# Sliding-window attention with a soft mixture of experts: P normalised at the head of the next round, in front of the masked copy, the store of x directly behind the bias

## The chip, the core and the metric

The kernel runs on one core of a Trainium2 chip. Its engines are TensorE (PE in the profile; its weight loads are PEld), VectorE (DVE), ScalarE (ACT), GpSimd (POOL) and SyncE (SP, which issues most DMAs). Each engine takes its own instructions in the order in which the program has them and waits on semaphores for the others. The metric is the time of one execution in microseconds (us), as the median of several runs; before the change it is 286.43 us (three runs, 285.88 to 286.63).

## What is computed

First causal attention with a window of 128 keys and a bias that falls linearly with distance, for 8 batches of 576 rows and 8 heads of 64 columns; then, with x the attention's output as 4608 rows of 512 columns, a soft mixture of 8 experts with 4 slots each.

```python
scores = scale * q @ k^T                           # scale = 1/8
scores = where(0 <= rel < 128, scores - slope[h] * rel, -1e9)
attn = exp(scores - max(scores))
attn = attn / (sum(attn) + 1e-9)                   # P
x = (attn @ v)                                     # to 4608 x 512

logits = x @ phi                                   # 32 slots
d = softmax over rows of logits                    # slot inputs: d^T @ x
slot_out[e] = relu(slot_input[e] @ w1[e]) @ w2[e]
return softmax over slots of logits @ slot_out
```

## The kernel before

**Rounds.** A batch's 576 rows are four tiles of 128 and one of 64. A full tile is worked in two groups of four heads, the tile of 64 in one. That makes 9 groups a batch and 72 in all (`groups`); `number` gives a group's place. The front part of the kernel is one loop with a round for each group (round 0 to round 71). It is a software pipeline: in round i the scores of group i+1 are multiplied, the softmax of group i is taken, group i-3 is transposed and group i-4 is multiplied with v. The order on every engine is the order of the code (`manual_schedule`); no scheduler moves anything.

**The steps of a round, by engine.** In the letters that the prediction uses:

- DVE: the masked copy **M** (`merge`, L286) folds the 192 score columns of a block of 64 rows to the 128 of the window. `rowmax` (L300), the reciprocal of the row sums of the group before (`inverse`, L313) and `bias` (L304, written b) follow. **N** (`normalise`, L317) multiplies the four 128x128 blocks of P, all in SBUF, by the reciprocals `rs`. **X** (`x_store`, L424) copies a finished tile of x from PSUM (`xp`) to SBUF. X occurs once a tile, so in about every second round.
- ACT: copy of the transposed P out of PSUM (`split`, L380), sometimes `x_keep` (L447), then the exponentials of the round's group (`expo`, L359), which wait for b.
- POOL: the row sums plus epsilon (`total`, L309), and two `affine_select` on the transposed P, **A** (L386, part that meets the previous tile's keys) and **B** (L388, own keys). Both read and write SBUF.
- PE: transposes (`flip`, L374), **V** (`values`, L410: first the part that needs A, then the part that needs B), scores of the next group (L261 and L270), and now and then the transposes of x, the logits and so on.

**The extra work.** Tiles are collected in passes of four. A pass adds, in the rounds behind it, some DVE work that stands at the end of a round, or in front of the next masked copy: `token_max` (L469), `token_sum` (L496, L498), `slots_max` (L536, L537) and `slot_add` (L522, L524).

**What sets the order around the change.** `softmax_front(new, old)` writes M, rowmax, inverse, b and N of a round, in this order. X and the extra work come later in the loop's body, so on DVE a round ends with N, then X where there is one, then the extra work. `xp` is one PSUM buffer: V of the next tile waits until X has read the last one. P has three SBUF buffers (`p4s`); the reciprocals are in tiles from a pool with two buffers. The first rounds are shorter in depth: `SKIP` is 7, and in round 7 no group is transposed.

Of the kernel before, what the change touches and what calls it, by code (L numbers as in the profile page):

```python
# [10 lines left out]
F32 = mybir.dt.float32  # L11
# [13 lines left out]
P = 128  # L25
# [20 lines left out]
SKIP = 7  # L46
# [18 lines left out]
def bc(ap, dim, n):  # L65
    ap = ap.unsqueeze(dim)
    shape = list(ap.shape)
    shape[dim] = n
    return ap.to_broadcast(shape)
# [3 lines left out]
def tile_attn_softmoe(  # L73
# [16 lines left out]
    work = ctx.enter_context(tc.tile_pool(name="work", bufs=2))  # L90
# [53 lines left out]
    st = {}  # L144
    last = B - 1

    def order(b):
        return (1, 2, 3, 4, 0) if b == last else range(NT)
# [13 lines left out]
    groups = [(b, t, g) for b in range(B) for t in order(b) for g in range(2 if t < 4 else 1)]  # L162
    number = {key: i for i, key in enumerate(groups)}
    n = len(groups)
# [111 lines left out]
    ALL, LO, HI = slice(0, 4), slice(0, 2), slice(2, 4)  # L276
    EVEN, ODD = slice(0, 4, 2), slice(1, 4, 2)

    def merge(key, us=ALL):
        x = ranges(key, us).rearrange("p a (x y) -> p a x y", y=KB)  # L280
        m = x.shape[1]
        if key[1] < 4:
            to, of, keep = x[:, :, 0:6:5], x[:, :, 2:4], bc(mask.bitcast(I32), 1, m)
        else:
            to, of, keep = x[:, :, 0:8:4], x[:, :, 2:8:4], bc(bc(mask[:, 0].bitcast(I32), 1, 2), 1, m)
        nc.vector.copy_predicated(to, keep, of)  # L286

    def ranges(key, us):
        if number[key] == 0:
            return st[key]["parts"][us.start // 2].unsqueeze(1)  # L290
        return st[key]["s4"]
# [4 lines left out]
    def rowmax(key, us):  # L296
        if "nb" not in st[key]:
            st[key]["nb"] = work.tile([P, 4], F32, tag="nb", name="nb")
        st[key]["mx"] = ranges(key, us)[:, :, 4 * P - 2:4 * P]
        nc.vector.tensor_reduce(st[key]["mx"], merged(key, us), axis=AX.X, op=ALU.max, negate=True)  # L300

    def bias(key, us):
        nb = st[key]["nb"][:, us].rearrange("p (a u) -> p a u", u=2)
        nc.vector.tensor_scalar_mul(nb, st[key]["mx"], SCALE)  # L304

    def total(key, us, eng=None):
        if "rs" not in st[key]:
            st[key]["rs"] = work.tile([P, 4], F32, tag="rs", name="rs")
        (eng or nc.vector).tensor_scalar(  # L309
            st[key]["rs"][:, us], st[key]["sm"][:, us], EPS, 1.0, op0=ALU.add, op1=ALU.mult)  # L310

    def inverse(key, us):
        nc.vector.reciprocal(st[key]["rs"][:, us], st[key]["rs"][:, us])  # L313

    def normalise(key, us):
        p4, rs = st[key]["p4"][:, us], st[key]["rs"][:, us]
        nc.vector.tensor_tensor(p4, p4, bc(rs, 2, P), op=ALU.mult)  # L317

    def normalise_first(key, us):
        p4 = st[key]["p4"]  # L320
        for u in range(4)[us]:
            nc.scalar.mul(p4[:, u], p4[:, u], st[key]["rs"][:, u:u + 1])  # L322
# [3 lines left out]
    def filler():  # L326
        if fillers:
            fillers.pop(0)()

    def softmax_front(new, old):  # L330
        first, eager = number[old] == 0, 0 < number[old] < EAGER
        merge(new)
        filler()
        if not eager:
            total(old, ALL, nc.gpsimd)
        if first:
            inverse(old, ALL)
            normalise_first(old, LO)
        rowmax(new, ALL)
        filler()  # L340
        if not first and not eager:
            inverse(old, ALL)
        filler()
        bias(new, ALL)
        if eager:
            total(old, ALL)
            inverse(old, ALL)
        filler()
        normalise(old, HI if first else ALL)

    def expo(key, us=ALL):
        s = st[key]
# [421 lines left out]
    with tc.manual_schedule(engines=ORDERED):  # L774
        scores(0)
        loads(0)
        for i in range(n):
            new = groups[i]
            run("pre", i)
            if i:  # L780
                softmax_front(new, groups[i - 1])
            else:
                for us in (LO, HI):
                    merge(new, us)
                    rowmax(new, us)
                    bias(new, us)
                    expo(new, us)
            near = int(i < SKIP)
            if i + near >= FLAG and i != SKIP:
                flip(groups[i + near - FLAG])  # L790
                split(groups[i + near - FLAG])
            run("act", i)
            if i + near >= LAG and i != SKIP:
                values(groups[i + near - LAG])
                after_values(i, groups[i + near - LAG])
            if i + 1 < n:
                scores(i + 1)
            if i + 1 < n - 1:
                loads(i + 1)
            if i:  # L800
                expo(new)
            run("pe", i)
            load_weights_at(i)
            run("dve", i)
# [23 lines left out]
        split(gc)  # L828
        token_exp(end)
        total(gd, LO)  # L830
        inverse(gd, LO)
        normalise(gd, LO)
# [296 lines left out]
```

## Time and profile before

| what | value |
|---|---|
| median of the runs | 286.43 us |
| the profiled execution, its own time | 286.09 us |
| its span, first to last instruction | 284.3 us |
| mean granted clock of TensorE | 0.992 |
| DVE / PE / ACT / POOL busy | 218.6 / 257.5 / 190.5 / 111.7 us |
| DMA, mean over the span | 255 GB/s |

The rounds 9 to 71 lie between 29.7 and 211.6 us; behind them come the last groups, the experts and the output. Times in rows of the trace are microseconds from the start of the span: start, duration, engine, line, operation, out<-in with shapes, count, and in brackets the idle time of the engine before the row with what ended it.

### The profile page before, as it was taken

Reading aid. Unit: us, or ns where it says so; the run is one execution under the profiler, and the core shown is the slowest. Engines: PE = TensorE matmul, PEld = TensorE weight load, DVE = VectorE, ACT = ScalarE, POOL = GpSimd, SP = SyncE. Lnnn points to the kernel's source line nnn. Section 1 sums busy time; section 2 is a strip of 40 time slices with the busy share of each in tenths; the row PEclk is TensorE's granted clock in tenths of the full one; section 3 lists DMA queues with packets and bytes.
Section 4 is the critical chain, followed back from the end, with each engine's and each line's share of the span. In section 5 each row is a group of like instructions: output and inputs, shape, how many; then the busy total and the mean of one; then the engine's idle time right before and its main releaser. Section 6 shows DMA issues by size and latency. Waiting matters only on the chain.

```text
span 284.3 us, 11675 instructions
## 1 busy us (share of the span) xinstructions
PE 257.5 (91%) x4575; PEld 180.7 (64%) x4575; DVE 218.6 (77%) x546; ACT 190.5 (67%) x780; POOL 111.7 (39%) x221
## 2 busy tenths in 40 slices
PE   7789898989899999998989998998989899999990
PEld 3567676767577677676667766766666443587750
DVE  1789998997998898899999899897973352656352
ACT  2868868887798887897897888887774411044460
POOL 3035734481574385265527526556452011000000
PEclk9999999999999999999999999999999999999996
DMA  5735368889786998889698778876565588999997
GB/s 167 238 110 153 115 173 250 255 247 295 252 277 184 303 303 262 257 265 285 221 298 283 255 236 280 268 212 218 166 213 199 172 257 296 417 416 373 376 357 295
DMA packets 36767, 72.49 MB, mean 255 GB/s; under 512 B 4413, under 2 KB 15337, under 8 KB 36713
## 3 DMA queue, kind: packets, MB, share of 16 engines
q1 hardware_dynamic: 35992, 71.25, 75.7%
q8 instruction: 36, 0.59, 0.8%
q10 hardware_dynamic: 720, 0.51, 0.6%
q14 instruction: 19, 0.15, 0.2%
HBM read 62.30 MB, written 9.44 MB: 252 GB/s over the span
## 4 chain that ended last, share of the span: by engine, by line
PE 44%; DVE 38%; ACT 9%; issue 3%; DMA 3%; POOL 1%; DVEq 0%; ACTq 0%; SPq 0%; POOLq 0%
DVE area L317 12%; DVE s L300 9%; PE xp L410 8%; ACT area L359 6%; PE op L967 5%; PE s L270 5%; DVE area L424 5%; PE hp L930 5%; DVE s L286 4%; PE po L992 4%; PE s L261 2%; PE lp L456 2%; PE pq L374 2%; DVE acc L522 2%; DMA area<-v_n 2%
## 5 line engine op out<-in xcount | busy, mean ns | idle before, releaser
L359 ACT ACTIVATE area<-s,nb 128x128 f32<-128x128 f32 x286 | 101.9, 379 | 21.6 <-DVE nb L304 20.2
L410 PE MATMUL xp<-area 128*64 128x128 f32 (+1 forms) x1104 | 71.7, 270 | 9.5 <-DVE area L424 6.6
L410 PEld LDWEIGHTS xp<-area 128*64 128x64 f32 x1104 | 54.5, 137 | 16.4 <-POOL area L388 5.0
L359 ACT ACTIVATION_READ_ACCUMULATOR area<-s,nb 128x1 f32 x286 | 62.2, 218 | 0.0
L317 DVE TENSOR_TENSOR area<-area,rs 128x512 f32<-128x512 f32 (+1 forms) x73 | 59.9, 821 | 1.7 <-ACT area L447 0.4
L270 PE MATMUL s<-kq 64*64 64x192 f32 (+2 forms) x1144 | 57.0, 316 | 0.0
L386 POOL TENSOR_SCALAR_AFFINE_SELECT area<-area 128x512 f32<-128x512 f32 (+1 forms) x57 | 42.7, 748 | 26.9 <-ACT area L380 26.3
L380 ACT COPY area<-pq 128x512 f32<-128x512 f32 (+1 forms) x72 | 42.5, 592 | 16.0 <-PE pq L374 14.3
L300 DVE TENSOR_REDUCE s<-s 128x4 f32<-128x512 f32 (+1 forms) x72 | 50.0, 694 | 2.2
L388 POOL TENSOR_SCALAR_AFFINE_SELECT area<-area 128x512 f32<-128x512 f32 (+1 forms) x57 | 46.5, 817 | 3.9
L270 PEld LDWEIGHTS s<-kq 64*64 64x64 f32 x1144 | 41.2, 139 | 3.4
L309 POOL TENSOR_SCALAR rs<-sm 128x4 f32<-128x4 f32 x70 | 13.5, 193 | 71.2 <-ACT area L359 69.8
L286 DVE COPY_PREDICATED s<-cst,s 128x256 f32<-128x256 int32 (+1 forms) x72 | 30.2, 419 | 4.8 <-PE s L270 4.4
L374 PE MATMUL pq<-unit_r,area 64*128 64x64 f32 x552 | 31.4, 234 | 1.9 <-ACT area L322 1.2
L374 PEld LDWEIGHTS pq<-unit_r,area 64*128 64x128 f32 x552 | 23.0, 140 | 11.6 <-issue 5.0
L261 PE MATMUL s<-ramp,pair_of 64*64 64x384 bf16 x286 | 27.0, 358 | 2.5 <-ACT area L359 2.0
L424 DVE COPY area<-xp 128x512 f32<-128x512 f32 (+1 forms) x38 | 24.1, 633 | 3.6 <-PE xp L410 3.4
L447 ACT COPY area<-pq 128x512 f32<-128x512 f32 x34 | 20.2, 594 | 0.3 <-PE pq L432 0.3
L261 PEld LDWEIGHTS <-pair_of 64*64 64x64 bf16 x288 | 9.5, 106 | 15.7 <-issue 12.0
L438 PEld LDWEIGHTS pq<-unit_r,area 64*128 64x128 f32 x264 | 10.7, 138 | 13.2 <-issue 11.7
L994 ACT COPY ob<-po 128x512 f32<-128x512 f32 x19 | 10.4, 592 | 11.4 <-PE po L992 11.4
L994 DVE COPY ob<-po 128x512 f32<-128x512 f32 x17 | 11.2, 686 | 6.6 <-PE po L992 4.4
(164 smaller groups left out, 276.6 us busy)
## 6 DMA issues: line engine op xcount, KB each, us to landing
w<-w SPq DMA_DIRECT2D x53, 512.0 KB, 5.4
out<-ob SPq DMA_DIRECT2D x36, 256.0 KB, 3.6
kq<-q_t SPq DMA_DIRECT2D x69, 128.0 KB, 3.3
kq<-k_t SPq DMA_DIRECT2D x32, 256.0 KB, 3.4
area<-v_n SPq DMA_DIRECT2D x31, 256.0 KB, 4.5
area<-w SPq DMA_DIRECT2D x8, 512.0 KB, 4.9
area<-v_n SPq DMA_DIRECT2D x12, 128.0 KB, 5.2
kq<-w SPq DMA_DIRECT2D x3, 512.0 KB, 5.6
```

Of the source, the lines that this page charges most:

```text
L261: nc.tensor.matmul(dst[strip], lhsT=pair_of[rows, int(t == 0), strip], rhs=src, start=True, stop=False)
L270: nc.tensor.matmul(parts[par][KB * jj:KB * jj + KB, second * u + KB * skip:second * u + WIN], lhsT=qt[rows, jj if t < 4 else j, KB * h:KB ...
L286: nc.vector.copy_predicated(to, keep, of)
L300: nc.vector.tensor_reduce(st[key]["mx"], merged(key, us), axis=AX.X, op=ALU.max, negate=True)
L317: nc.vector.tensor_tensor(p4, p4, bc(rs, 2, P), op=ALU.mult)
L359: nc.scalar.activation(s["p4"][:, u], src, AF.Exp, bias=s["nb"][:, u:u + 1], scale=SCALE, accum_out=s["sm"][:, u:u + 1],)
L374: nc.tensor.transpose(s["pt"][:, 2 * (u % 2) + u // 2, r], s["p4"][rows, u], ident[rows, rows])
L380: nc.scalar.copy(pa[:, us].rearrange("p u (r w) -> p u r w", r=2), s["pt"][:, us])
L386: nc.gpsimd.affine_select(prev, own, [[-step, m], [0, 4], [-1, KB]], ALU.is_gt, 0.0, base=-i0, channel_multiplier=1)
L388: nc.gpsimd.affine_select(own, own, [[step, m], [0, 4], [1, KB]], ALU.is_ge, 0.0, base=i0, channel_multiplier=-1)
L410: nc.tensor.matmul(xp[D * par:D * par + D, j, 0:w], lhsT=v_slot[b, t - 1 + ph][:, D * h:D * h + D], rhs=src[:, :, par, i] if t < 4 else sr ...
L424: nc.vector.tensor_copy(dst, src[:, :, 0:w])
```

## The change

From round 9 on, N of group i-2 stands at the head of round i, in front of the masked copy, in place of the end of the round before. So X and the extra work of a round come directly behind b, and N follows them. Round 8 has no N for this reason; round 71 has two, one at its head and one at its end. The reciprocals get a third buffer, since they are read later.

```diff
     def total(key, us, eng=None):
         if "rs" not in st[key]:
-            st[key]["rs"] = work.tile([P, 4], F32, tag="rs", name="rs")
+            st[key]["rs"] = work.tile([P, 4], F32, tag="rs", name="rs", bufs=3)
...
     def softmax_front(new, old):
         first, eager = number[old] == 0, 0 < number[old] < EAGER
+        late = number[new] > SKIP
+        if number[new] > SKIP + 1:
+            normalise(groups[number[old] - 1], ALL)
         merge(new)
         filler()
...
             inverse(old, ALL)
         filler()
-        normalise(old, HI if first else ALL)
+        if not late or number[new] == n - 1:
+            normalise(old, HI if first else ALL)
```

The order of the instructions of PE, ACT, POOL and SP is what it was. On DVE, rows change places only where X or extra work stands between N and the next masked copy: in 42 of the rounds 9 to 70. In the other 20, N keeps its place between b and the next M. Lines behind the change have numbers higher by 4 (X is L428, `token_sum` L500 and L502, `slots_max` L540 and L541).

On DVE, the end of round 9, the first place that differs. Names: `nb` is the bias, `rs` the reciprocals, `area` holds P and x, `s_0` and `s_1` are the two score buffers. Before:

```order
L313 RECIPROCAL rs<-rs 128x4
L304 TENSOR_SCALAR nb<-s_1_84 128x4
L317 TENSOR_TENSOR area<-area,rs 128x512
L424 COPY area<-xp 128x512
L286 COPY_PREDICATED s_0_83<-cst,s_0_83 128x2x2x64
```

With the change:

```order
L313 RECIPROCAL rs<-rs 128x4
L304 TENSOR_SCALAR nb<-s_1_84 128x4
L428 COPY area<-xp 128x512
L317 TENSOR_TENSOR area<-area,rs 128x512
L286 COPY_PREDICATED s_0_83<-cst,s_0_83 128x2x2x64
```

N and X have changed places; the masked copy stands behind both as before.

On DVE, the end of round 14, where extra work follows X (`sb` sums of the token softmax, `dp` a PSUM tile that PE writes, `cm` the slot maxima, `ln` the logits by slot). Before:

```order
L304 TENSOR_SCALAR nb<-s_0_83 128x4
L317 TENSOR_TENSOR area<-area,rs 128x512
L424 COPY area<-xp 128x512
L498 COPY fine<-sb 128x1
L536 TENSOR_REDUCE cm<-dp 128x4
L537 TENSOR_TENSOR ln<-dp,cm 128x4x32
L286 COPY_PREDICATED s_1_84<-cst,s_1_84 128x2x2x64
```

With the change:

```order
L304 TENSOR_SCALAR nb<-s_0_83 128x4
L428 COPY area<-xp 128x512
L502 COPY fine<-sb 128x1
L540 TENSOR_REDUCE cm<-dp 128x4
L541 TENSOR_TENSOR ln<-dp,cm 128x4x32
L317 TENSOR_TENSOR area<-area,rs 128x512
L286 COPY_PREDICATED s_1_84<-cst,s_1_84 128x2x2x64
```

N has moved past four instructions, one of which reads what PE has just written.

On DVE, the end of round 29, where X and the token maximum (`nm`, of the logits `lg` that ACT copies) stand behind N. Before:

```order
L304 TENSOR_SCALAR nb<-s_1_84 128x4
L317 TENSOR_TENSOR area<-area,rs 128x512
L424 COPY area<-xp 128x512
L469 TENSOR_REDUCE nm<-lg 128x1
L286 COPY_PREDICATED s_0_83<-cst,s_0_83 128x2x2x64
```

With the change:

```order
L304 TENSOR_SCALAR nb<-s_1_84 128x4
L428 COPY area<-xp 128x512
L473 TENSOR_REDUCE nm<-lg 128x1
L317 TENSOR_TENSOR area<-area,rs 128x512
L286 COPY_PREDICATED s_0_83<-cst,s_0_83 128x2x2x64
```

Here N has moved past two instructions that wait, X for PE and the maximum for ACT.

## The prediction

> **What bounds the kernel now.** First the page: the span, then the chain that ended last.
>
> ```profile
> span 284.3 us, 11675 instructions
> PE 44%; DVE 38%; ACT 9%; issue 3%; DMA 3%; POOL 1%; DVEq 0%; ACTq 0%; SPq 0%; POOLq 0%
> ```
>
> The chain goes to and fro between PE and DVE. The change acts in rounds 9 to 71, so the second view is the busy time in that window, and the third the waits in it.
>
> ```profile
> 29.67:211.60 181.93, 170.79 (x3350) 124.61 (x3346) 165.45 (x405) 148.75 (x650) 97.11 (x181) 1.00 0.77 243
> PE xp L410 <- DVE area L424: 6.6, 11, 1.0
> PE xp L410 <- DVE fine L496: 0.8, 1, 0.8
> PE xp L410 <- POOL lg L489: 0.8, 1, 0.8
> DVE area L424 <- PE xp L410: 3.4, 5, 0.8
> DVE nm L469 <- ACT lg L464: 2.8, 3, 1.1
> DVE s L286 <- PE s L270: 2.4, 6, 1.3
> DVE cm L536 <- PE dp L502: 1.1, 3, 0.4
> ```
>
> Of 181.9 us PE is busy for 170.8 and DVE for 165.5. PE has 11.1 us to give and no more; most of it is V (L410) waiting for X (L424), 6.6 us in 11 rounds. I count the two single waits of 0.8 with them (a row of round 14 below shows one: V starts at 47.39, 0.14 behind the end of X at 47.25, and the profile names an instruction that ended nearby). That makes 8.2 us in 13. DVE's busy time is not all work, which the group of N shows:
>
> ```profile
> L317 DVE TENSOR_TENSOR area<-area,rs 128x512 f32<-128x512 f32 x64 | 53.9, 843 | 1.4 <-ACT area L447 0.4
> 49.08 0.69 DVE L317 TENSOR_TENSOR area<-area,rs 128x512 f32<-128x512 f32 x1
> 49.69 0.42 DVE L286 COPY_PREDICATED s<-cst,s 128x256 f32<-128x256 int32 x1
> 31.00 1.12 DVE L317 TENSOR_TENSOR area<-area,rs 128x512 f32<-128x512 f32 x1
> 32.04 0.68 DVE L424 COPY area<-xp 128x512 f32<-128x512 f32 x1
> 30.92 0.66 POOL L386 TENSOR_SCALAR_AFFINE_SELECT area<-area 128x512 f32<-128x512 f32 x1 [0.27 <-ACT area L380]
> 31.65 0.99 POOL L388 TENSOR_SCALAR_AFFINE_SELECT area<-area 128x512 f32<-128x512 f32 x1
> 200.90 1.18 DVE L317 TENSOR_TENSOR area<-area,rs 128x512 f32<-128x512 f32 x1
> L388 POOL TENSOR_SCALAR_AFFINE_SELECT area<-area 128x512 f32<-128x512 f32 x52 | 42.9, 825 | 3.5
> ```
>
> Alone, N takes 0.69 and the next instruction starts 0.61 behind it; its mean is 0.843. At 31.00 it starts 0.08 behind A (30.92) and ends 1.20 behind A's start; B, 0.66 alone, is stretched to 0.99 in turn. So N and the selects exclude each other: N runs for its 0.69 from 0.50 behind A's start. The Trainium skill, "SBUF — State Buffer", section "SBUF: two separate sides", has this as a lock: a DVE instruction with two SBUF inputs and a GpSimd one that reads SBUF share a port, and the first to start holds it to its end. The rows agree in kind, but the hold ends 0.16 before A's record does.
>
> **The change part by part.** No instruction is added or removed, and PE, ACT, POOL and SP keep their orders. The third `rs` buffer costs nothing: it adds no instruction, and N is the last reader of a buffer two rounds old. N reads P two rounds before PE transposes it, now one round before; the shortest rounds are 1.9 us long (M to M, 47.75 to 49.69), so there is time, and I cost that at nothing (if it were late, the transpose would wait, at most by N's 0.69). 42 N move, 20 keep their place. Three terms.
>
> *1. The lock.* Row by row, N over 0.69 comes to 6.45 us in the 42 moved N, from 0.43 at 31.00 to 0.49 at 200.90. Twelve carry 5.4 of it: in six, other work besides X or in X's place stands between (2.7 us), in six X alone (2.7 us). The end of round 14 stands for the first six:
>
> ```profile
> 45.49 1.15 DVE L317 TENSOR_TENSOR area<-area,rs 128x512 f32<-128x512 f32 x1
> 46.57 0.68 DVE L424 COPY area<-xp 128x512 f32<-128x512 f32 x1
> 47.54 0.29 DVE L537 TENSOR_TENSOR ln<-dp,cm 128x128 f32<-128x128 f32 x1
> 45.45 0.66 POOL L386 TENSOR_SCALAR_AFFINE_SELECT area<-area 128x512 f32<-128x512 f32 x1 [0.27 <-ACT area L380]
> 46.18 0.99 POOL L388 TENSOR_SCALAR_AFFINE_SELECT area<-area 128x512 f32<-128x512 f32 x1
> 47.39 0.33 PE L410 MATMUL xp<-area 128*64 128x128 f32 x2 [0.78 <-POOL lg L489]
> ```
>
> X and the extra work take 0.60 + 0.58 from 46.57 to the masked copy at 47.75 (its record: 0.29 at 47.54 less an overlap of 0.08). With X at 45.49, N would start near 46.7, past A and in all but the last of an unhindered B (46.18 to 46.84): the whole 0.46 is saved. I take all 2.7. In the X-only six, N starts 0.60 behind where it did, 0.68 behind A's start. By then A has let go (0.50) and B starts at 0.73: a tie within 0.05. If N is first, 0.43 to 0.50 is saved; if B is, N ends at 0.73 + 0.50 + 0.69, and nothing is. I take half, 1.35, and half of the other 1.07, together **-4.5 us**; bounds 0 and -6.45.
>
> *2. The cover that N gave.* Where X or the extra work waits, N ran in that wait. Now the wait comes first and N is paid behind it, in front of M:
>
> ```profile
> 87.62 0.69 DVE L317 TENSOR_TENSOR area<-area,rs 128x512 f32<-128x512 f32 x1
> 89.06 0.69 DVE L424 COPY area<-xp 128x512 f32<-128x512 f32 x1 [0.75 <-PE xp L410]
> 89.66 0.28 DVE L469 TENSOR_REDUCE nm<-lg 128x1 f32<-128x129 f32 x1
> 90.03 0.43 DVE L286 COPY_PREDICATED s<-cst,s 128x256 f32<-128x256 int32 x1
> 41.77 0.69 DVE L317 TENSOR_TENSOR area<-area,rs 128x512 f32<-128x512 f32 x1
> 43.53 0.29 DVE L469 TENSOR_REDUCE nm<-lg 128x1 f32<-128x129 f32 x1 [1.07 <-ACT lg L464]
> 92.91 0.29 DVE L536 TENSOR_REDUCE cm<-dp 128x4 f32<-128x128 f32 x1 [0.39 <-PE dp L502]
> 51.29 0.69 DVE L317 TENSOR_TENSOR area<-area,rs 128x512 f32<-128x512 f32 x1
> 52.13 0.69 DVE L424 COPY area<-xp 128x512 f32<-128x512 f32 x1
> ```
>
> At 89.06 X starts when V ends, whatever N does; M then comes 0.61 later. The waits count five such X, two maxima (the third is hidden under a wait of M for PE, the 1.3 above) and three `cm`; with two X that wait 0.15 or less (52.13 is the first) that is 12 x 0.61 = **+7.3 us** if PE and ACT are no earlier. Behind the waiting instruction stand N and M, and for M wait rowmax, the bias and ACT's exponentials.
>
> *3. PE's lead.* X starts at b where its tile is ready, so V starts earlier, at most 8.2 us in 13 rounds, and brings the ends of the waits of term 2 forward. But V's second half needs B, and N now delays B:
>
> ```profile
> 82.44 0.86 DVE L317 TENSOR_TENSOR area<-area,rs 128x512 f32<-128x512 f32 x1
> 83.22 0.68 DVE L424 COPY area<-xp 128x512 f32<-128x512 f32 x1
> 82.71 1.11 POOL L386 TENSOR_SCALAR_AFFINE_SELECT area<-area 128x512 f32<-128x512 f32 x1
> 83.89 0.66 POOL L388 TENSOR_SCALAR_AFFINE_SELECT area<-area 128x512 f32<-128x512 f32 x1
> 84.04 1.22 PE L410 MATMUL xp<-area 128*64 128x128 f32 x16 [0.64 <-DVE area L424]
> 32.87 0.41 PE L410 MATMUL xp<-area 128*64 128x128 f32 x3 [0.87 <-DVE area L424]
> ```
>
> At 82.44, X first would end at 83.1 and A, unhindered, at 83.37: V could start 0.64 earlier. N then ends near 83.9, B, held, 0.53 behind it (as 47.17 is behind 46.64) at 84.4 in place of 84.55. V's second half gains 0.13 to 0.2 of the 0.64. At 31.00, X would end at 31.7 and N at 32.3, B at 32.85, and V's second half 0.6 behind its start still begins with it: V ends near 33.45 in place of 33.96, 0.5 of 0.87. Rounds 14 and 23, where N moves out of B's way, give back all 0.78. I take 0.6 of 8.2, **-4.9 us**; bounds 0 and -8.2.
>
> *Sum.* -4.5 + 7.3 - 4.9 = **-2.1 us**. What follows the rounds starts when they end and keeps its order, so the gain passes through. Against the profiled execution's 286.09 us that is 284.0; the median of the runs lies 0.34 above that execution: **284.3 us**.
>
> **The rivals.**
>
> *N wins the ties.* In the six X-only rounds N is first and saves all 2.7 in place of 1.35: -3.5, **282.9 us**. For it: N's place at 0.68 is ahead of B's 0.73. Against it: A's place is not always the same (at 82.44 it starts 0.27 behind N, so a moved N meets A itself), and where V ends late, X and N shift. By the page named above the first to start would hold the port, so N, if it is first by 0.05: then this rival's sum, 282.9, holds.
>
> *The ties are lost.* B is first each time: term 1 is -3.15, the sum -0.7, **285.7 us**, which is no change that a measurement of this kernel can tell (about 0.3%, 0.9 us). For it: an X that starts 0.1 late decides it, and at 89.06 and 52.13 X does wait for V. Against it: at 31.00 and 45.49 X's tile is ready before N is done, without a wait in its row.
>
> *Slower: POOL swallows the lead.* N, later, holds the port while B wants it; V's second half waits for B and PE ends as late as before. Term 3 is then 13 x 0.07 = -0.9 and the sum -4.5 + 7.3 - 0.9 = +1.9, **288.3 us**. It decides from a lead of (7.3 - 4.5) / 13 = 0.22 us a wait; the two worked examples have 0.13 to 0.2 and 0.5, so it is not far.
>
> **How the numbers follow.** Forecast 284.3: 0.37, own range 283.2 to 285.4. N wins the ties: 0.18. Ties lost, or the pipeline takes up what it is given elsewhere: 0.23. POOL swallows the lead: 0.22. Faster by over 0.3% is the first two, 0.55; within 0.3%, 0.23; slower, 0.22. The bounds of the terms together reach from -6.45 + 7.3 - 8.2 = -7.35 to +7.3, but their ends go badly together: the tie that saves N's time is the one that holds B back and costs PE its lead. The range, 281.8 to 288.2, takes in the ties won with some more lead, and half of the slower case.
>
> **What would show it.** Right: N's mean falls from 0.843 towards 0.77, V's wait for X from 6.6 us to under 3, and X and the maxima show more waiting on DVE than 3.4 and 2.8 us, less than 0.61 more each. In the end of round 14 N is 0.69, and round 15 starts over 1 us earlier, with round 9's gain. Wrong: A stays at 0.66 but B's mean grows past the 825 ns that it has in this window and V waits for B (then the slower rival), or N's mean stays over 0.8 (ties lost). What would make the prediction wrong altogether is a stage behind the rounds that does not start earlier when they end earlier.

## The result, and the profile after

The changed kernel takes 283.63 us (median of six runs, 282.77 to 284.39), the kernel before 286.06 beside it. The ratio is 0.9928 with a 95% interval of 0.9904 to 0.9953: the change gains 0.5 to 1.0%. The profiled execution took 283.76 us in place of 286.09.

The page of the changed kernel, its span and the chain that ended last by engine:

```profile
span 282.0 us, 11653 instructions
PE 56%; DVE 22%; ACT 7%; POOL 6%; issue 4%; DMA 2%; DVEq 0%; ACTq 0%; POOLq 0%
```

DVE's share of the chain has gone from 38% to 22%, PE's from 44% to 56%, POOL's from 1% to 6%. Next the busy times (PE, PEld, DVE, ACT, POOL) in the stretch of the prediction's second view, from M of round 9 to 3.0 us behind M of round 71, and some of the waits there, each with its total, count and longest:

```profile
29.62:208.90 179.28, 171.53 (x3350) 124.49 (x3346) 160.64 (x405) 148.31 (x650) 93.55 (x181) 1.00 0.79 249
```

```profile
DVE area L428 <- PE xp L414: 6.3, 10, 1.4
DVE nm L473 <- ACT lg L468: 3.6, 3, 1.4
PE xp L414 <- POOL area L392: 2.7, 8, 0.4
DVE cm L540 <- PE dp L506: 2.6, 5, 0.7
DVE s L286 <- PE s L270: 1.4, 4, 0.9
PE xp L414 <- POOL area L390: 1.2, 2, 0.9
```

The stretch has become 2.65 us shorter (181.93 to 179.28), with the same count of instructions on every engine. PE's idle time in it fell from 11.1 to 7.75 us. V's wait for X, 6.6 us before, has gone from the list (nothing over 0.1), and so have the two single waits of 0.8. V now waits for B (L392) and A (L390) instead, 3.9 us. DVE does what was foreseen of it: X, the token maximum and `cm` wait longer (3.4 to 6.3, 2.8 to 3.6, 1.1 to 2.6), and M waits less for PE (2.4 to 1.4).

The groups of V, N, B and A in the same stretch of the changed kernel, and in a second fence those of V and A before, which the prediction did not show:

```profile
L414 PE MATMUL xp<-area 128*64 128x128 f32 (+1 forms) x1024 | 66.7, 269 | 4.1 <-POOL area L392 2.7 <-POOL area L390 1.2
L317 DVE TENSOR_TENSOR area<-area,rs 128x512 f32<-128x512 f32 x64 | 52.3, 817 | 0.1
L392 POOL TENSOR_SCALAR_AFFINE_SELECT area<-area 128x512 f32<-128x512 f32 x52 | 41.4, 796 | 3.5
L390 POOL TENSOR_SCALAR_AFFINE_SELECT area<-area 128x512 f32<-128x512 f32 x51 | 34.2, 670 | 16.7 <-ACT area L384 16.2
```

```profile
L410 PE MATMUL xp<-area 128*64 128x128 f32 (+1 forms) x1024 | 65.6, 269 | 9.3 <-DVE area L424 6.6 <-DVE fine L496 0.8 <-POOL lg L489 0.8
...
L386 POOL TENSOR_SCALAR_AFFINE_SELECT area<-area 128x512 f32<-128x512 f32 x51 | 38.6, 758 | 22.2 <-ACT area L380 21.6
```

N fell from 843 to 817 ns only and B from 825 to 796, but A from 758 to 670 (alone it takes 0.66): what is left of the lock is mostly between N and B. V's idle time fell by 5.2 us (9.3 to 4.1), but its own time grew by 1.1 (65.6 to 66.7): a V that has to stop between its halves takes 0.66 twice (round 9 below), one that need not takes 1.09 (round 14). Three places of the timeline show it. First round 9:

```profile
30.87 0.66 POOL L390 TENSOR_SCALAR_AFFINE_SELECT area<-area 128x512 f32<-128x512 f32 x1 [0.27 <-ACT area L384]
30.98 0.69 DVE L428 COPY area<-xp 128x512 f32<-128x512 f32 x1
31.59 0.68 DVE L317 TENSOR_TENSOR area<-area,rs 128x512 f32<-128x512 f32 x1
31.60 1.19 POOL L392 TENSOR_SCALAR_AFFINE_SELECT area<-area 128x512 f32<-128x512 f32 x1
31.87 0.66 PE L414 MATMUL xp<-area 128*64 128x128 f32 x8
32.19 0.42 DVE L286 COPY_PREDICATED s<-cst,s 128x256 f32<-128x256 int32 x1
32.84 0.66 PE L414 MATMUL xp<-area 128*64 128x128 f32 x8 [0.31 <-POOL area L392]
```

This is the tie, and N wins it by 0.01 us (31.59 against 31.60): N takes 0.68, B 1.19. V starts 0.20 behind the end of X, and its second half (32.84) waits 0.31 for the B that N has held up. Round 11 is the tie lost:

```profile
36.15 0.69 DVE L428 COPY area<-xp 128x512 f32<-128x512 f32 x1 [0.27 <-PE xp L414]
36.58 0.66 POOL L392 TENSOR_SCALAR_AFFINE_SELECT area<-area 128x512 f32<-128x512 f32 x1
36.76 1.02 DVE L317 TENSOR_TENSOR area<-area,rs 128x512 f32<-128x512 f32 x1
```

X waits 0.27 for V, so B is first and N takes 1.02. Of the six rounds with X alone whose stretch the prediction shared out by halves (9, 11, 36, 43, 52, 63), N is at 0.68 in two (9 and 63), and at 0.87 to 1.17 in the other four. Round 14, with extra work behind X:

```profile
45.28 0.66 POOL L392 TENSOR_SCALAR_AFFINE_SELECT area<-area 128x512 f32<-128x512 f32 x1
45.65 1.09 PE L414 MATMUL xp<-area 128*64 128x128 f32 x16
45.69 0.29 DVE L541 TENSOR_TENSOR ln<-dp,cm 128x128 f32<-128x128 f32 x1
45.90 0.68 DVE L317 TENSOR_TENSOR area<-area,rs 128x512 f32<-128x512 f32 x1
46.49 0.42 DVE L286 COPY_PREDICATED s<-cst,s 128x256 f32<-128x256 int32 x1
```

N meets neither select (it starts 0.62 behind B and takes its 0.68), and V, which started at 47.39 before, starts at 45.65, both halves in one piece.

How much earlier M of a round starts (after less before, from the timelines):

| round | 9 | 15 | 24 | 30 | 44 | 56 | 71 | end of the span |
|---|---|---|---|---|---|---|---|---|
| us | -0.05 | -1.26 | -1.09 | -1.07 | -2.20 | -2.46 | -2.67 | -2.3 |

### The profile page after: what moved, and what is told of

Read it like the earlier page. It is cut to its first block, busy times and chain, and to the rows that moved or that the text cites. A ratio compares the mean times of both kernels' runs of the same rounds, so it can differ in the third digit from the quotient of the medians.

```text
span 282.0 us, 11653 instructions
## 1 busy us (share of the span) xinstructions
PE 256.9 (91%) x4575; PEld 179.0 (63%) x4575; DVE 214.0 (76%) x546; ACT 190.1 (67%) x780; POOL 108.2 (38%) x221
## 4 chain that ended last, share of the span: by engine, by line
PE 56%; DVE 22%; ACT 7%; POOL 6%; issue 4%; DMA 2%; DVEq 0%; ACTq 0%; POOLq 0%
PE xp L414 13%; PE s L270 8%; DVE s L300 6%; DVE area L317 6%; PE op L971 5%; ACT area L363 5%; PE hp L934 5%; PE pq L378 4%; PE s L261 4%; PE po L996 4%; DVE s L286 3%; POOL area L392 3%; PE lp L460 3%; POOL area L390 2%; DVE acc L526 2%
## 5 line engine op out<-in xcount | busy, mean ns | idle before, releaser
L414 PE MATMUL xp<-area 128*64 128x128 f32 (+1 forms) x1104 | 72.9, 271 | 4.3 <-POOL area L392 2.7
L317 DVE TENSOR_TENSOR area<-area,rs 128x512 f32<-128x512 f32 (+1 forms) x73 | 58.5, 801 | 0.3
L270 PE MATMUL s<-kq 64*64 64x192 f32 (+2 forms) x1144 | 55.6, 311 | 0.1
L390 POOL TENSOR_SCALAR_AFFINE_SELECT area<-area 128x512 f32<-128x512 f32 (+1 forms) x57 | 38.2, 670 | 22.5 <-ACT area L384 20.5
L392 POOL TENSOR_SCALAR_AFFINE_SELECT area<-area 128x512 f32<-128x512 f32 (+1 forms) x57 | 45.1, 790 | 3.9
L309 POOL TENSOR_SCALAR rs<-sm 128x4 f32<-128x4 f32 x70 | 15.4, 220 | 76.5 <-ACT area L363 70.6
L270 PEld LDWEIGHTS s<-kq 64*64 64x64 f32 x1144 | 39.7, 136 | 3.7 <-DMA kq<-k_t 0.5
L378 PE MATMUL pq<-unit_r,area 64*128 64x64 f32 x552 | 31.5, 233 | 3.4 <-ACT area L322 2.3
L378 PEld LDWEIGHTS pq<-unit_r,area 64*128 64x128 f32 x552 | 23.1, 140 | 13.2 <-issue 3.9
L428 DVE COPY area<-xp 128x512 f32<-128x512 f32 (+1 forms) x38 | 24.2, 636 | 6.9 <-PE xp L414 6.3
L261 PE MATMUL s<-ramp,pair_of 64*64 64x384 bf16 x286 | 26.1, 350 | 3.3 <-ACT area L363 2.4
L261 PEld LDWEIGHTS <-pair_of 64*64 64x64 bf16 x288 | 9.3, 104 | 16.2 <-issue 11.9
L442 PEld LDWEIGHTS pq<-unit_r,area 64*128 64x128 f32 x264 | 10.7, 137 | 13.8 <-issue 11.3
L998 ACT COPY ob<-po 128x512 f32<-128x512 f32 x19 | 10.4, 592 | 11.4 <-PE po L996 10.5
```

Of the source, the lines that this page charges most:

```text
L261: nc.tensor.matmul(dst[strip], lhsT=pair_of[rows, int(t == 0), strip], rhs=src, start=True, stop=False)
L270: nc.tensor.matmul(parts[par][KB * jj:KB * jj + KB, second * u + KB * skip:second * u + WIN], lhsT=qt[rows, jj if t < 4 else j, KB * h:KB ...
L378: nc.tensor.transpose(s["pt"][:, 2 * (u % 2) + u // 2, r], s["p4"][rows, u], ident[rows, rows])
L390: nc.gpsimd.affine_select(prev, own, [[-step, m], [0, 4], [-1, KB]], ALU.is_gt, 0.0, base=-i0, channel_multiplier=1)
L392: nc.gpsimd.affine_select(own, own, [[step, m], [0, 4], [1, KB]], ALU.is_ge, 0.0, base=i0, channel_multiplier=-1)
L414: nc.tensor.matmul(xp[D * par:D * par + D, j, 0:w], lhsT=v_slot[b, t - 1 + ph][:, D * h:D * h + D], rhs=src[:, :, par, i] if t < 4 else sr ...
```

## The experiments

Three questions were open: what the lock costs in time and not in busy time; whether the cover that N gave is worth 7.3 us; and what POOL gives back. From here on "rounds" is the time from M of round 9 to M of round 71 and "tail" what follows to the end of the span, both of the one profiled execution. Ahead of round 9 the order on DVE is the same in the six kernels of the table below, and yet M of round 9 starts up to 1.5 us apart (28.21 to 29.67), so kernels are compared by their rounds and by the medians of their runs.

**The lock taken away, in both orders** (`nosel_before`, `nosel_after`). These two kernels, and the two behind them, leave the masking by A and B out of what V reads, so they do not compute the attention and serve for their times alone. In `split`:

```diff
-        if t:
+        pp = pa
+        if False:
```

> The order of before; the two GpSimd selects on the transposed P (A and B) are left out, and V reads the unselected copy for both of its parts. Lock theory: N has no partner on the shared port in most rounds, its mean falls from 0.843 us to about 0.70, and V never waits for B. The time falls by some part of the 9.2 us that N was stretched by in rounds 9 to 70: 279 to 283 us. Rival (DVE's stretch was slack of a loop that PE sets): the time stays within 1 us of the kernel before.

> The changed order with the same two selects left out. To be held against the run before it. If the gain of the change is the lock alone (N moved out of the way of A and B), the two are equal or this one is slower by the cover lost, 0 to +3 us. If it is PE's lead (V no longer waits for X) and X's closer place behind the bias, this one stays faster by 1 to 3 us, since V has no B to wait for.

**The lock kept, but V not waiting for the selects, in both orders** (`idle_before`, `idle_after`). The second select writes the tile of the first, and V reads neither:

```diff
-                own, own, [[step, m], [0, 4], [1, KB]], ALU.is_ge, 0.0, base=i0, channel_multiplier=-1)
-        s.update(pd=pa, pp=pp)
+                prev, own, [[step, m], [0, 4], [1, KB]], ALU.is_ge, 0.0, base=i0, channel_multiplier=-1)
+        s.update(pd=pa, pp=pa)
```

> The order of before; A and B run as they did, but B writes beside (where A writes) and V reads the unselected copy for both parts, so that V waits for neither A nor B. N is stretched by A and B as before (mean about 0.84 us). Held against the run without selects (279.3 us) it prices the stretch of N by itself: if DVE's lost time is what counts, this is 284 to 286 us; if it is V's waiting for A and B, 279 to 281 us.

> The changed order with A and B idle in the same way. Held against the run before it: if the change gains because N is stretched less on DVE (2.4 us in the moved N), this is faster by 1.5 to 3 us, as the change itself was; if it gains because A is no longer held up by N and V starts earlier, this is within 0.7 us, as without the selects.

Measured, with the real kernels in the first row:

| | order before: median, rounds | changed order: median, rounds | the change: median, rounds |
|---|---|---|---|
| V waits for A and B | 286.06, 178.9 | 283.63, 176.3 | -2.4, -2.6 |
| selects run, V does not wait | 284.29, 177.0 | 279.09, 171.6 | -5.2, -5.4 |
| no selects | 279.25, 173.6 | 279.03, 171.8 | -0.2, -1.8 |

The idle pair, each from M of its round 9 to 3.0 us behind M of its round 71 (busy times as above), the first kernel with its largest wait of V and its N, the second with its waits of X and the maximum and its N:

```profile
28.73:208.75 180.02, 169.53 (x3350) 124.21 (x3346) 164.87 (x405) 148.94 (x650) 97.70 (x181) 1.00 0.78 246
```

```profile
PE xp L410 <- DVE area L424: 7.0, 11, 1.3
```

```profile
L317 DVE TENSOR_TENSOR area<-area,rs 128x512 f32<-128x512 f32 x64 | 53.6, 838 | 1.3 <-ACT area L447 0.4
```

```profile
29.64:204.19 174.55, 169.51 (x3350) 125.24 (x3346) 158.32 (x405) 147.99 (x650) 95.45 (x181) 1.00 0.80 255
```

```profile
DVE area L428 <- PE xp L414: 4.7, 7, 0.9
DVE nm L473 <- ACT lg L468: 3.9, 3, 1.6
```

```profile
L317 DVE TENSOR_TENSOR area<-area,rs 128x512 f32<-128x512 f32 x64 | 50.8, 794 | 0.1
```

In the order of before, N with the lock is 838 ns and V waits 7.0 us for X; without the selects (next rows, `nosel_before`, the same stretch) N is 699 ns and V still waits 4.2.

```profile
PE xp L411 <- DVE area L425: 4.2, 9, 0.8
```

```profile
L317 DVE TENSOR_TENSOR area<-area,rs 128x512 f32<-128x512 f32 x64 | 44.7, 699 | 1.6 <-DVE nb L304 0.4
```

`nosel_before`, `nosel_after` and `idle_before` came out within one of the cases named for them; `idle_after` did not, being 5.2 us faster than its partner where 1.5 to 3 or under 0.7 was expected.

Three things follow. First, with the order of before the selects cost 5.0 us though V does not wait for them (284.29 against 279.25; 3.4 in the rounds). With the changed order they cost nothing (279.09 against 279.03; -0.2 in the rounds), although N is still stretched to 794 ns. Both idle kernels have the same PE work (169.53 and 169.51 us); what differs is PE's idle time, 10.5 us (180.02 less 169.53) against 5.0 (174.55 less 169.51), and no wait of V for X is listed in the second. So what the stretch cost was PE's wait. Second, without any lock the order is worth less: 0.2 us by the medians, 1.8 in the rounds of one execution, whose tail is 0.9 longer; how much of the 1.8 reaches the end is not settled. Third, where V does wait for the selects, the change gains 2.6 in the rounds and not 5.4. V's dependence on A and B costs 1.9 us in the order of before (178.9 less 177.0) and 4.7 in the changed one (176.3 less 171.6): the difference, **2.8 us, is given back** through A and B.

**N left in front where the maximum waits** (`cover`), and the reverse, **N moved in those rounds only** (`only_max`). They are the eight rounds 13, 22, 29, 38, 45, 54, 61 and 67, whose work on DVE includes `token_max`:

```diff
-        late = number[new] > SKIP
-        if number[new] > SKIP + 1:
+        late = number[new] > SKIP and not waits(number[new])
+        if number[new] > SKIP + 1 and not waits(number[new] - 1):
```

(`only_max` has the two lines without `not`.)

> The changed kernel, but in the eight rounds with a token maximum (13, 22, 29, 38, 45, 54, 61, 67) N stands where it was before, in front of X and of the maximum, so that it covers their waits again. Cover theory: in the trace of the change these rounds wait 8.6 us in front of X and the maximum; N (0.61 each) goes back into the wait in rounds 13, 22, 29, 45, 61 in full and in 38 and 54 in part, 1.5 to 3.5 us faster than the change, some of it taken by PE: about 282 us on the scale of 283.6. Rival (PE sets these rounds anyway): within 0.7 us of the change.

> The kernel before, with N moved in those eight rounds with a token maximum alone. Cover theory: slower than before by 8 x 0.61 us less what PE had to wait for DVE anyway and less the one round hidden under a load: +2 to +4 us (288 to 290). Rival (the cover is worth nothing because PE sets these rounds): within 0.9 us of before.

`cover` takes 283.68 us (0.9909 of the kernel before beside it, 0.9877 to 0.9941): it keeps the cover in eight rounds and is no faster than the change. `only_max` takes 286.53 (1.0018, 0.9993 to 1.0042): it gives the cover up in eight rounds and is 0.4 us slower by the medians, which is not clear of the noise. M of round 30 starts 0.86 us late in its trace, as the cover would have it, but M of round 44 starts 0.29 early: here a DVE that was late by one N is on time again some rounds on. The theory of the cover as a sum of 0.61 a wait misses both times.

**The change split in two.** N moved in the 18 rounds in which it took 0.79 us or more and had something to pass (`stretched`), and in the other 24 of the 42 (`unstretched`, with `not in`):

```diff
+    stretched = {9, 11, 14, 18, 23, 27, 34, 36, 43, 46, 47, 52, 55, 56, 63, 64, 66, 68}
...
-        late = number[new] > SKIP
-        if number[new] > SKIP + 1:
+        late = number[new] > SKIP and number[new] in stretched
+        if number[new] > SKIP + 1 and number[old] in stretched:
```

> The kernel before, with N moved only in the 18 rounds (9 to 68) in which the trace of before shows N stretched by over 0.1 us and X or extra work behind it; in the other 24 it stands in front as before. Theory (PE waits for X because a stretched N stands in front of it; the rest of the moves is worth nothing): the whole gain of the change, 283 to 284.2 us. Rival (X directly behind the bias gains everywhere, N stretched or not): about half, 284.6 to 285.4.

> The complement: N moved only in the other 24 rounds, among them all twelve in which X, the maximum or cm waits. Theory: within 0.9 us of the kernel before (286.2), on the slower side if anything. Cover as the prediction priced it (12 x 0.61): 288 us or more. Rival (X directly behind the bias gains everywhere): 285 us or less.

`stretched` takes 283.43 us (0.9905 of 285.55, 0.9874 to 0.9937; rounds 176.4): the whole gain. `unstretched` takes 288.92 (1.011, 1.0066 to 1.0154; rounds 181.0): a loss of 3.4 us by the medians and 2.1 in the rounds. That is outside the 0.9 us of the theory put on record for it, and above the 288 us given there for the cover, though far from all of 12 x 0.61. Waits of `unstretched` between its M of rounds 9 and 71, and the end of its round 29:

```profile
DVE area L430 <- PE xp L416: 9.5, 9, 1.4
PE xp L416 <- DVE area L430: 5.3, 9, 1.0
```

```profile
90.20 0.69 DVE L430 COPY area<-xp 128x512 f32<-128x512 f32 x1 [1.43 <-PE xp L416]
90.81 0.28 DVE L475 TENSOR_REDUCE nm<-lg 128x1 f32<-128x129 f32 x1
91.00 0.83 DVE L317 TENSOR_TENSOR area<-area,rs 128x512 f32<-128x512 f32 x1
91.75 0.42 DVE L286 COPY_PREDICATED s<-cst,s 128x256 f32<-128x256 int32 x1
```

Here is the term of the cover: X waits 1.43 for V, and N, which ran in that wait before, is paid in front of M. In this kernel, where V still waits 5.3 us for X elsewhere, it shows in the time. The same 24 moves on top of the 18 cost nothing that shows: 283.63 with them, 283.43 without. The two parts do not add: -2.6 and +2.1 in the rounds alone, -2.6 together.

**One input of N out of SBUF** (`psum_after`). The reciprocals of groups 7 to 69 are written into the group's score tile in PSUM, to the columns that held the row maxima:

```diff
+        if psum:
+            st[key]["rp"] = st[key]["mx"]
+            nc.vector.reciprocal(st[key]["rp"], st[key]["rs"].rearrange("p (a u) -> p a u", u=2))
...
+            nc.vector.tensor_tensor(p4, p4, bc(st[key]["rp"], 3, P), op=ALU.mult)
```

> The changed kernel, with the reciprocals of groups 7 to 69 written to the two free columns of the score bank in PSUM, so that N has one SBUF input only. If two SBUF inputs are what makes N and the selects exclude each other, N's mean falls from 0.80 to about 0.70 and A and B to 0.66 each. If that lock is what still costs time, 280 to 282.5 us; if PE alone sets the rounds by now, within 0.9 us of the change (283.6); if the score matmuls, which now wait for the reciprocal in their bank, are held up, slower.

It takes 313.97 us (1.0973, 1.0911 to 1.1036). Its groups of N, B and A and two of its waits, all over the whole span:

```profile
L322 DVE TENSOR_TENSOR area<-area,s 128x512 f32<-128x512 f32 x63 | 43.2, 685 | 28.1 <-PE s L270 27.6
L400 POOL TENSOR_SCALAR_AFFINE_SELECT area<-area 128x512 f32<-128x512 f32 (+1 forms) x57 | 38.1, 668 | 3.9
L398 POOL TENSOR_SCALAR_AFFINE_SELECT area<-area 128x512 f32<-128x512 f32 (+1 forms) x57 | 37.7, 662 | 33.6 <-ACT area L392 33.6
```

```profile
PE s L261 <- DVE s L315: 29.1, 39, 1.6
...
DVE area L322 <- PE s L270: 27.6, 39, 1.0
```

The lock is gone from all three (685, 668 and 662 ns). The Trainium skill, "SBUF — State Buffer", section "SBUF: two separate sides", counts a DVE instruction as a holder of the port shared with GpSimd when two of its inputs are in SBUF or when it runs in a 2-port mode, and says that `tensor_tensor` (N) has no such mode; these rows agree. But the scores of a later group go to the tile in which the reciprocals stand, and PE waits 29.1 us for the reciprocal (L315) and N 27.6 for the scores. A version with the reciprocals in a bank of their own was not tried.

**N directly behind X, in front of the extra work** (`behind_x`). No N at the head of a round; in the loop, behind the part that holds X:

```diff
+            if SKIP < i < n - 1:
+                normalise(groups[i - 1], ALL)
```

> As the change, but N stands directly behind X (or behind the bias where a round has no X), in front of the extra work: it covers the waits of the maximum in rounds 13, 22, 67 and of cm in 30, 39, 62 again, and in rounds 14, 23, 46, 55, 64, 68 it falls back among A and B. Lock theory: 0.46 us lost in each of these six, 1 to 2.5 us slower than the change. Cover theory: 6 x 0.61 won back, 1 to 3 us faster than the change. If neither is on the path: within 0.7 us.

Ten runs scatter from 282.58 to 289.5 us; the seven up to 286.51 have a median of 284.89 (0.9944, 0.9908 to 0.998). The rounds of its profiled execution, 283.02 us, are 176.4, those of the change. Whether it is slower is not settled, so neither the lock theory nor the other two is told apart by it.

**Two buffers of reciprocals in place of three** (`rs2`, without `bufs=3`):

> The changed kernel with two buffers for the reciprocals in place of three. Theory: equal to the change within 0.7 us, since N is done with a buffer before it is written again. Rival: the sums of the next group wait for N, slower.

283.57 us (0.991, 0.9879 to 0.994), the time of the change. The third buffer neither costs nor gains anything that shows, as the prediction costed it.

No version beats the change by more than the intervals; `stretched` equals it.

## Why the prediction was right, and where its steps were not

The time was right, 284.3 forecast and 283.63 measured; of the three terms one was right. The sum came out because the errors of the other two cancel, which is luck: the 4.5 us of term 1 were for the most part in term 3 already, and term 2 had 7.3 us where PE's waits outside V grew by 1.5.

**Term 3, PE's lead: right.** Forecast -4.9. V's waits for X went from 8.2 us to none (the two waits of 0.8 went with the others, as counted), and V got 3.9 us of waits for B and A in their place: -4.3. That N would hold B and take a part of the lead back is the slower rival's mechanism, and it is there, in the waits and in the 2.8 us by which the change gains less than the idle pair. It is a part and not the whole: the rival had 0.07 us left of each wait, the trace has 0.33 (4.3 / 13). B's mean fell, against the sign that the prediction named for this rival, while V's wait for B grew (0.3 to 2.7); the sign to read is the wait, since a stretched B can only cost where V waits for it.

**Term 1, the lock: mis-sized, and mostly the same loss as term 3.** Forecast -4.5. On the rows that the step looked at it was near: the six rounds with other work behind b saved 2.3 of their 2.7 us, the six with X alone 1.4 of 2.7, all 18 stretched rounds 3.9 of 6.4. What it put at nothing are the other 24 moved N, of which two met a select before, by a little, and twelve do now: they have 1.7 us over 0.69 where they had 0.1. In round 29, N at 87.62 ran in a gap in front of A (88.76) before; in the changed kernel it starts at 88.20, inside B. The timelines of DVE and POOL of the changed kernel there:

```profile
88.01 0.28 DVE L473 TENSOR_REDUCE nm<-lg 128x1 f32<-128x129 f32 x1
88.20 0.83 DVE L317 TENSOR_TENSOR area<-area,rs 128x512 f32<-128x512 f32 x1
```

```profile
87.84 0.66 POOL L392 TENSOR_SCALAR_AFFINE_SELECT area<-area 128x512 f32<-128x512 f32 x1
```

So the 42 moved N saved 2.2 us, and the mean went to 817 ns and not towards 770. But the size is not the main error. `idle_after` has N at 794 ns and costs what `nosel_after` costs with no lock at all. The stretch counted in the time because N stood in front of X while PE waited for `xp`: DVE's lost time and PE's wait are in the main one loss, seen on two engines, and the prediction added it twice.

**Term 2, the cover: mis-sized.** Forecast +7.3 for twelve waits. The places were right: X waits 2.9 us more, the maximum 0.8, `cm` 1.5. `only_max` is 0.4 us slower with eight rounds moved, `unstretched` 2.1 to 3.4 with 24, among them all twelve waits. `unstretched` also gained some lead (V's waits for X are 6.9 us in place of 8.2) and its N lost time to B (0.83 in round 29), so the price of a wait alone is not measured; but twelve times 0.61, a price read from single rounds, is too much even there. With the lead (`stretched` against the change) it is nothing measurable. The likely reason, not tried by itself, is that a DVE that is 0.6 late in a round has time in hand in the next, because PE sets the pace there; the prediction's "if PE and ACT are no earlier" was the condition, and it was not met.

**What the sum should have been.** PE's alone, as the trace has it afterwards. V's idle time in front of it went from 9.3 to 4.1 us and its own time from 65.6 to 66.7, together -4.1, which is term 3 less what B and A took back. The idle time in front of the transposes and the scores' bias (L378, L442, L261) went from 1.1 to 2.6, +1.5. That is -2.6 against the -2.65 measured, with no term for DVE at all. Whether the +1.5 is the lost cover as PE feels it was not followed.

**The signs.** N of round 14 is 0.68 and round 15 starts 1.26 us earlier, as forecast; V's wait for X is gone, and X and the maximum wait more, by less than 0.61 each. But N's mean stayed over 0.8 (0.817), which was the sign for the lost ties. In four of the six rounds N was stretched, and yet the time did not come to the 285.7 us of that rival: N now stands behind X, so that its stretch no longer makes V wait for X. The gain passes through the stage behind the rounds but for 0.3 to 0.4 us (-2.67 at M of round 71, -2.3 at the end); from the start of the last matmuls to the end of the span it is 10.1 us before and 10.5 after. The tail of `idle_after` is 1.4 us longer than that of its partner. It lies between M of round 71 and the experts' first matmul, 22.6 us where the kernel before and the changed one have 21.2: the granted clock there was 0.92 (1.00 in those two), and this execution, 280.35 us, is the slowest of its six. So it does not belong to the change.

**Not tried:** a kernel in which V waits for A and not for B, and a second PSUM buffer for `xp`. So what V's dependence on the selects costs is not split between A and B other than by the waits in the changed kernel, 1.2 and 2.7.

## What to carry to other kernels

Make the sum on the engine that sets the pace, in its own waits: a stretched instruction on another engine costs what it makes that engine wait, and counting both counts it twice. A wait that an instruction used to cover need not cost its full price: here 24 moves that lost 2.1 to 3.4 us alone lost nothing together with the 18 others; test both halves of such a change apart, because they need not add. When two engines exclude each other, ask of each new order who waits for the one that now loses.

## What the runs showed of the hardware

- N directly behind b starts 0.14 to 0.19 us behind b's start (62 of the 63 rounds of the kernel before; the other waits), while X in its place starts 0.08 behind it in the median of the 25 rounds of the changed kernel in which no wait is listed (0.04 to 0.29). N reads the reciprocal that stands right in front of b, X reads nothing of the kind; which of their differences makes it was not tried. Where nothing else waits this is a small gain that the prediction did not have.
- The order decides by hundredths: N at 31.59 beside B at 31.60 gets the port and B takes 1.19; N at 36.76, 0.18 behind B, takes 1.02. In the 26 places of the kernel before (29 to 212 us) in which N starts 0.01 to 0.5 us behind the start of a select that takes 0.66, N ends 1.19 or 1.20 behind the select's start: what the loser pays is fixed by the other's start.
